# Split heads of a decay attention: two TensorE passes for the products with v in place of three, row sums on VectorE, squares on ScalarE

## Chip, core and metric

The kernel runs on one core of a Trainium2 chip. A core has a matrix engine (TensorE, PE in the profile, with its weight loads as PEld), a vector engine (VectorE, DVE), an engine for pointwise functions (ScalarE, ACT), a general one (GpSimd, POOL) and one that issues transfers (SyncE, SP). Each works through its own queue in order; semaphores tie the queues together. Data lies in SBUF (128 partitions) or in PSUM, where TensorE writes its sums, eight banks of 128 x 512 fp32. The metric is the time of one execution in microseconds.

## Reference

Eight batches of eight heads, 576 positions of 64 values. Each head is causal attention whose scores get a decay: the difference of cumulated logarithms of f. The 4608 rows of 512 that come out go through a two-layer MLP with a squared relu.

```python
scores = scale * np.matmul(q, k.transpose(0, 1, 3, 2))
cum = np.cumsum(np.log(np.clip(f, 0.0001, 1.0)), axis=-1)
scores = np.where(causal, -1e9, scores + cum[:, :, :, None] - cum[:, :, None, :])
scores = scores - np.max(scores, axis=-1, keepdims=True)
attn = np.exp(scores)
attn = attn / (np.sum(attn, axis=-1, keepdims=True) + 1e-09)
x = np.matmul(attn, v)                 # heads side by side: 4608 x 512
h = np.maximum(x @ w_in, 0.0)          # 512 -> 2048
out = h * h @ w_out                    # 2048 -> 512
```

## The kernel before

**Precision.** Most products run in a faster fp32 format of TensorE (F32R) that rounds its operands. To keep the digits, an operand is split into a rounded upper part and a lower part, the rest: ph and pl for the exponentials p, vh and vl for v, xh and xl, gh and gl in the MLP. A product of two split operands takes three passes: upper by upper, upper by lower, lower by upper.

**Heads.** The first 14 heads (`NWHOLE`) multiply unsplit fp32; in that time the weights of the MLP are loaded and split. The other 50 are **split heads**. A head has six units (`UNITS`): blocks of 128 keys (64 for the last) against the queries that see them, with 320, 320, 192, 64, 448 and 256 queries. The loop at the end of the kernel goes through slots, one unit of one head each. In a slot stand, in this order, the score of the unit, the products with v of the unit two slots earlier (`LAG`), and whatever is due there: parts of the next head's preparation (`prep`, `split_v`), its row maxima (`max_units`), and halves of MLP steps, dealt out by `fill`. A half is `mlp1` (12 matmuls of 256 columns into bank 4) or `mlp2` (6 matmuls of 512). Most batches' heads get 64 halves for the 48 slots of eight heads, one batch's 96: four or six steps to a head.

**A unit's way.** `score` multiplies on TensorE and takes the exponential on ScalarE (p); GpSimd masks the block on the diagonal (L384; units 1 to 5 have one); `split_p` rounds p to ph on ScalarE (L397) and subtracts on VectorE to get pl (L398); `av_split` multiplies with v. The 576 queries are summed in two parts, upper (320 columns, units 0 to 4) and lower (256 columns, units 5 and 4), each in the same PSUM bank 0, one after the other. A part's last matmul is followed on ScalarE by a copy of x (L444) and one of the row sum den (L446), which comes from a column of ones in vh. When both have read the bank, the next sum may start there.

**Division.** `finish` spreads the row sums of two heads over the partitions by way of DRAM, inverts them on VectorE (L462, L463) and has GpSimd multiply x (L471).

**MLP step.** ScalarE takes the relu r (L509), VectorE squares it to g (L510), ScalarE squares it to gh, rounded (L511), VectorE subtracts to get gl (L512); `mlp2` uses them a step later. r and g have one buffer each.

**Order.** `in_order` ties every engine's instructions to the order in which the program writes them, SP's DMAs from the first slot on. So what an instruction waits for also holds up all that stands behind it on its engine.

## Time and profile before

| what | us |
|---|---|
| median of 3 runs | 1231.75 (1227.86 to 1232.46) |
| the profiled execution's own time | 1235.45 |
| its span, first to last instruction | 1233.7 |
| first score of a split head | 214.2 |
| stretch with MLP steps alone | from 1081.8 on |
| TensorE, VectorE, ScalarE, GpSimd busy in the span | 1185.7, 772.9, 701.1, 410.9 |

How to read the rows in what follows. A row of a timeline has start and duration in us, engine, line of the kernel, operation, tiles (written <- read), shapes, and in brackets how long the engine sat idle before it and what ended the wait. A row of groups has busy time and mean duration in ns, then the idle time before and its releasers. The row of a window has, for each engine, the busy time within it and the number of instructions, then TensorE's granted clock, the DMA share and GB/s. Matmuls overlap, so a matmul's cost is the distance from its start to the next one's, not its duration; an engine's other instructions overlap a little too.

### The profile page before, as it was taken

How to read it: one execution, taken by the hardware profiler on the slowest of the kernel's cores; microseconds unless marked ns; L12 is line 12 of the kernel's file. 1: busy time of each engine (PE TensorE's matmuls, PEld its weight loads, DVE VectorE, ACT ScalarE, POOL GpSimd, SP SyncE). 2: the span in 40 equal slices, each digit the busy share in tenths (PEclk: the TensorE clock that was granted, in tenths of full speed). 3: DMA queues.
4: the chain of work that ended last, by engine and by line, in shares of the span. 5: the costliest groups of instructions: out<-in, count | busy, mean ns of one | idle time of the engine just before them, and what ended most of it. 6: DMA issues, size and time to landing. Idle time of an engine off the chain costs nothing.

```text
span 1233.7 us, 23332 instructions
## 1 busy us (share of the span) xinstructions
PE 1185.7 (96%) x7652; PEld 1050.8 (85%) x7652; DVE 772.9 (63%) x2044; ACT 701.1 (57%) x1720; POOL 410.9 (33%) x670
## 2 busy tenths in 40 slices
PE   5876998999999999999999999999999999999998
PEld 3554887988999899999899989998999899999997
DVE  7666874667676767666655676667666667533332
ACT  3553664666666666665655666666666666633332
POOL 4554544433333333332222233334333434200000
PEclk9897998999999999999999999999999999999999
DMA  7776531112121212121102121211121212000000
GB/s 202 180 158 159 165 103 43 36 40 50 42 58 41 57 33 53 32 58 36 49 16 58 27 58 42 57 34 48 36 58 42 58 41 58 12 27 1 18 18 18
DMA packets 114977, 71.62 MB, mean 58 GB/s; under 512 B 96908, under 2 KB 96908, under 8 KB 114856
## 3 DMA queue, kind: packets, MB, share of 16 engines
q1 hardware_dynamic: 113736, 66.00, 21.7%
q0 software_dynamic: 1120, 4.13, 1.6%
q8 instruction: 61, 1.00, 0.4%
q14 instruction: 60, 0.49, 0.1%
HBM read 59.90 MB, written 9.87 MB: 57 GB/s over the span
## 4 chain that ended last, share of the span: by engine, by line
PE 64%; ACT 2%; issue 1%; POOL 1%; DVE 0%; DMA 0%; SPq 0%; POOLq 0%; DVEq 0%
PE bank L501 25%; PE bank L524 24%; PE bank L407 3%; PE bank L372 2%; PE bank L409 2%; PE bank L324 2%; PE bank L408 2%; PE bank L369 2%; ACT den L446 0%; ACT r L509 0%; ACT p L382 0%; DMA den<-rdr 0%; ACT ph L397 0%; POOL v L310 0%; ACT gh L511 0%
## 5 line engine op out<-in xcount | busy, mean ns | idle before, releaser
L524 PE MATMUL bank<-w,gh 128*128 128x512 f32 x1152 | 414.7, 401 | 0.0
L501 PE MATMUL bank<-xh,w 128*128 128x256 f32 x2304 | 331.8, 287 | 2.8 <-DVE tcol L330 2.2
L501 PEld LDWEIGHTS bank<-xh,w 128*128 128x128 f32 x2304 | 302.9, 190 | 11.3 <-DVE tcol L330 2.4
L398 DVE TENSOR_TENSOR pl<-p,ph 128x320 fp32r<-128x320 f32 (+4 forms) x300 | 182.2, 607 | 201.7 <-ACT ph L397 192.9
L524 PEld LDWEIGHTS bank<-w,gh 128*128 128x128 f32 x1152 | 217.7, 189 | 38.5
L524 PE MATMUL bank<-w,gl 128*128 128x512 f32 x576 | 227.1, 394 | 0.1
L509 ACT ACTIVATE r<-bank 128x256 f32<-128x256 f32 x288 | 110.5, 384 | 198.7 <-PE bank L501 185.7
L510 DVE TENSOR_TENSOR g<-r 128x256 f32<-128x256 f32 x288 | 129.1, 448 | 145.1 <-ACT r L509 144.4
L384 POOL TENSOR_SCALAR_AFFINE_SELECT p<-p 128x128 f32<-128x128 f32 (+1 forms) x250 | 81.3, 325 | 413.8 <-ACT p L382 273.4
L397 ACT CAST ph<-p 128x320 fp32r<-128x320 f32 (+4 forms) x300 | 124.5, 415 | 151.6 <-POOL p L384 149.8
L501 PE MATMUL bank<-xl,w 128*128 128x256 f32 x1152 | 185.1, 283 | 0.0
L501 PEld LDWEIGHTS bank<-xl,w 128*128 128x128 f32 x1152 | 159.0, 191 | 0.0
L330 DVE CUSTOM_DVE_ANT_0 bank<-bank,mz 128x256 f32<-128x256 f32 (+4 forms) x320 | 133.1, 433 | 35.3 <-PE bank L324 29.4
L382 ACT ACTIVATE p<-bank 128x320 f32<-128x320 f32 (+4 forms) x300 | 116.1, 387 | 63.1 <-PE bank L372 51.3
L512 DVE TENSOR_TENSOR gl<-g,gh 128x256 fp32r<-128x256 f32 x288 | 126.0, 438 | 35.1 <-PE bank L524 0.5
L324 PE MATMUL bank<-rk 66*128 66x320 f32 (+9 forms) x384 | 111.8, 322 | 22.9 <-DMA rk<-qkraw 9.9
L511 ACT ACTIVATE gh<-r 128x256 fp32r<-128x256 f32 x288 | 120.6, 419 | 9.1
L524 PEld LDWEIGHTS bank<-w,gl 128*128 128x128 f32 x576 | 109.3, 190 | 14.2 <-DVE gl L512 0.9
L210 POOL TENSOR_TENSOR w<-osb,w 128x128 fp32r<-128x128 f32 x128 | 72.7, 596 | 79.4 <-ACT w L206 42.3
L407 PE MATMUL bank<-pl,vh 128*65 128x320 f32 (+4 forms) x350 | 96.8, 277 | 2.4 <-ACT den L446 2.4
L324 PEld LDWEIGHTS bank<-rk 66*128 66x128 f32 (+3 forms) x384 | 69.8, 189 | 33.4 <-issue 13.1
L408 PE MATMUL bank<-ph,v 128*64 128x320 f32 (+4 forms) x350 | 94.7, 270 | 0.0
(82 smaller groups left out, 1560.9 us busy)
## 6 DMA issues: line engine op xcount, KB each, us to landing
qkraw<-in_qk SPq DMA_DIRECT2D x50, 288.0 KB
v<-in_v SPq DMA_DIRECT2D x62, 160.0 KB
out<-osb SPq DMA_DIRECT2D x36, 256.0 KB
den<-rdr SPq DMA_DIRECT2D x62, 144.0 KB
w<-in_w_in SPq DMA_DIRECT2D x16, 512.0 KB
w<-in_w_out SPq DMA_DIRECT2D x16, 512.0 KB
rk<-in_qk POOLq DMA_DIRECT2D x14, 288.0 KB, 5.0
rl<-in_qk SPq DMA_DIRECT2D x14, 288.0 KB
```

The source lines that it names most:

```text
L324: nc.tensor.matmul(ps[:m, :n], st["r2"][:rows, q0:q0 + m], st["kl0"][:rows, k0:k0 + n], start=True, stop=True,)
L330: nc.vector.tensor_tensor_reduce(out=ps[:m, :n], in0=ps[:m, :n], in1=mz[:m, mo:mo + n], op0=ALU.add, op1=ALU.min, scale=-1.0, scalar=init, ...
L382: nc.scalar.activation(out=p[:kn, :n], in_=ps[:kn, :n], func=AF.Exp, scale=SCALE)
L397: nc.scalar.copy(out=ph[:, :n], in_=p[:, :n])
L398: nc.vector.tensor_tensor(out=pl[:, :n], in0=p[:, :n], in1=ph[:, :n].bitcast(F32), op=ALU.subtract,)
L407: nc.tensor.matmul(acc[:D + 1, o], vh, pl[:, i], start=first, stop=False)
L408: nc.tensor.matmul(acc[:D, o], vl, ph[:, i], start=False, stop=False)
L501: nc.tensor.matmul(ph[:, :T], w[:, s, cc], x[:, cc, :], start=(cc == 0 and k == 0), stop=(cc == NCC - 1 and k == 2),)
L510: nc.vector.tensor_tensor(out=g, in0=r, in1=r, op=ALU.mult)
L511: nc.scalar.activation(out=gh, in_=r, func=AF.Square)
L512: nc.vector.tensor_tensor(out=gl, in0=g, in1=gh.bitcast(F32), op=ALU.subtract)
L524: nc.tensor.matmul(po, g[:, ts], w[:, s], start=(fc == 0 and k == 0), stop=(fc == NF - 1 and k == 2),)
```

## The change

In split heads the split v lies side by side in one tile of 128 columns, `vhl`: columns 0 to 63 the upper part, 64 to 127 the lower. One matmul of these 128 columns with ph gives upper by upper in partitions 0 to 63 of the bank and lower by upper in 64 to 127; a second one, of the upper 64 columns with pl, adds to the first 64. At the end ScalarE copies partitions 64 to 127 to x, and VectorE adds partitions 0 to 63 to it.

The column of ones has no room any more, so the row sums are taken on VectorE: `sum_p` adds each unit's p into one tile (wmag), and after the last unit a transposing reduce adds it up over groups of 32 partitions. `store_sums` and `finish` bring the four groups together by way of DRAM. In every MLP step g is squared on ScalarE. Tiles move for the space: v has two buffers in place of three, den one, and the whole heads' row sums go to a free row of qkraw.

```diff
@@ split_v @@
-            vh = st["vh"] = vhs[h % 2]
-            st["vl"] = wk.tile([P, NJ, D], F32R, name="v", bufs=3)
-            nc.vector.tensor_copy(out=vh[:, :, :D], in_=vr)
+            v = st["vhl"] = vhls[h % 2]
+            nc.vector.tensor_copy(out=v[:, :, :D], in_=vr)
             nc.gpsimd.tensor_tensor(
-                out=st["vl"], in0=vr, in1=vh[:, :, :D].bitcast(F32), op=ALU.subtract,
+                out=v[:, :, D:], in0=vr, in1=v[:, :, :D].bitcast(F32), op=ALU.subtract,
             )
@@ split_p @@
         st["p"][u] = ph, pl
+        sum_p(h, u, p)
+
+    def sum_p(h, u, p):
+        st = state[h]
+        _, q0, q1 = UNITS[u]
+        if u == 0:
+            st["sum"] = wk.tile([P, S], F32, name="wmag", bufs=1), q1
+        total, known = st["sum"]
+        if known < q1:
+            o = slice(max(q0, known), q1)
+            nc.vector.tensor_tensor(
+                out=total[:, o], in0=total[:, o], in1=p[:, o.start - q0:q1 - q0], op=ALU.add,
+            )
+        if q0 < known:
+            nc.vector.tensor_copy(out=total[:, q0:min(known, q1)], in_=p[:, :min(known, q1) - q0])
+        st["sum"] = total, min(known, q0)
+        if u == NU - 1:
+            st["sums"] = wk.tile([P, NC], F32, name="sums")
+            nc.vector.tensor_reduce(
+                out=st["sums"], in_=total.rearrange("p (i c) -> p c i", c=NC),
+                axis=mybir.AxisListType.X, op=ALU.add, apply_transpose=True,
+            )
+
+    def store_sums(h):
+        st, i = state[h], h % 2
+        st["sdr"] = state[h - 1]["sdr"] if i else dr.tile([4, D, NC], F32, name="sdr")
+        nc.sync.dma_start(out=st["sdr"][:, i * 32:(i + 1) * 32], in_=st["sums"])
@@ av_split @@
-        nc.tensor.matmul(acc[:D + 1, o], vh, pl[:, i], start=first, stop=False)
-        nc.tensor.matmul(acc[:D, o], vl, ph[:, i], start=False, stop=False)
-        nc.tensor.matmul(acc[:D + 1, o], vh, ph[:, i], start=False, stop=last)
+        vhl = st["vhl"][:, j]
+        high = acc[:, o], vhl, ph[:, i]
+        low = acc[:D, o], vhl[:, :D], pl[:, i]
+        for k, args in enumerate((high, low) if first else (low, high)):
+            nc.tensor.matmul(*args, start=first and k == 0, stop=last and k == 1)
@@ av_part @@
+            if h >= NWHOLE:
+                nc.scalar.copy(out=x, in_=acc[D:, :n])
+                nc.vector.tensor_tensor(out=x, in0=x, in1=acc[:D, :n], op=ALU.add)
+                return
             nc.scalar.copy(out=x, in_=acc[:D, :n])
@@ finish @@
+            if h >= NWHOLE:
+                nc.sync.dma_start(
+                    out=st["cmp"].rearrange("p (g c) -> p g c", g=4),
+                    in_=st["sdr"].rearrange("g p c -> p g c"),
+                )
@@ mlp1 @@
         nc.scalar.activation(out=r, in_=ph[:, :T], func=AF.Relu)
-        nc.vector.tensor_tensor(out=g, in0=r, in1=r, op=ALU.mult)
+        nc.scalar.activation(out=g, in_=r, func=AF.Square)
         nc.scalar.activation(out=gh, in_=r, func=AF.Square)
@@ slots @@
+            at((h + 1) * NU, 1, store_sums, h)
```

Names keep their meaning; line numbers grow, so that L309 (cast of v) becomes L312, L310 (its lower part) L313, L398 (pl) L401, L444 (copy of x) L481, L512 (gl) L570. L416 and L420 are the adds and copies of `sum_p`, L425 its reduce, L482 the add from PSUM.

VectorE around the end of a split head, before: from pl of unit 4 to pl of the next head's unit 0.

```order
L398 TENSOR_TENSOR pl<-p,ph 128x448
L309 CAST vh_73<-v 128x5x64
L398 TENSOR_TENSOR pl<-p,ph 128x256
L510 TENSOR_TENSOR g<-r 128x256
L512 TENSOR_TENSOR gl<-g,gh 128x256
L290 CAST rk_68<-qkraw 64x576
L291 CAST rk_68<-qkraw 64x576
L398 TENSOR_TENSOR pl<-p,ph 128x320
```

The same place in VectorE's queue with the change:

```order
L401 TENSOR_TENSOR pl<-p,ph 128x448
L416 TENSOR_TENSOR wmag<-wmag,p 128x320
L420 COPY wmag<-p 128x128
L312 CAST vhl_73<-v 128x5x64
L401 TENSOR_TENSOR pl<-p,ph 128x256
L416 TENSOR_TENSOR wmag<-wmag,p 128x128
L420 COPY wmag<-p 128x128
L425 TENSOR_REDUCE sums<-wmag 128x18
L570 TENSOR_TENSOR gl<-g,gh 128x256
L482 TENSOR_TENSOR xt_9325<-xt_9325,bank_10166 64x320
```

The cast of v now stands behind an add and a copy, and the first add from PSUM behind a copy, an add and the reduce of unit 5. GpSimd's queue is as it was: the lower part of v, then the mask of unit 5.

ScalarE from the rounding of a head's unit 5 to the copy that reads the bank of the lower part, before:

```order
L397 CAST ph<-p 128x256
L509 ACTIVATE r<-bank_10187 128x256
L511 ACTIVATE gh<-r 128x256
L382 ACTIVATE p<-bank_10214 128x320
L444 COPY xt_9222<-bank_10051 64x320
L446 COPY den<-bank_10051 1x320
L292 CAST rl<-qkraw 64x576
L397 CAST ph<-p 128x320
L509 ACTIVATE r<-bank_10235 128x256
L511 ACTIVATE gh<-r 128x256
L382 ACTIVATE p<-bank_10256 128x320
L444 COPY xt_9222<-bank_10262 64x256
```

ScalarE's queue there with the change, from the first relu on:

```order
L567 ACTIVATE r<-bank_10307 128x256
L568 ACTIVATE g<-r 128x256
L569 ACTIVATE gh<-r 128x256
L385 ACTIVATE p<-bank_10334 128x320
L481 COPY xt_9325<-bank_10166 64x320
L296 CAST rl<-qkraw 64x576
L400 CAST ph<-p 128x320
L567 ACTIVATE r<-bank_10357 128x256
L568 ACTIVATE g<-r 128x256
L569 ACTIVATE gh<-r 128x256
L385 ACTIVATE p<-bank_10378 128x320
L481 COPY xt_9325<-bank_10384 64x256
```

Two squares (L568) have come into this stretch and one den copy (L446) has left it; a second den copy has left from behind the last row, and in its stead VectorE's L482 is the last to read the bank.

More of the change, by code (lines that the diff above doesn't have):

```diff
@@ L112, in decay_attention_relu2_kernel @@
     whole = [wk.tile([P, 2, S], F32, name="rl") for _ in range(2)]
-    vhs = [cpool.tile([P, NJ, D + 2], F32R, name=f"vh_{i}") for i in range(2)]
+    vhls = [cpool.tile([P, NJ, P], F32R, name=f"vhl_{i}") for i in range(2)]
+    qkraw = cpool.tile([P, 2, S], F32, name="qkraw")
+    NC = S // 32
     def f32(x):
@@ L237, in load @@
     def load(h):
-        raw = wk.tile([P, 2, S], F32, name="qkraw", bufs=1)[:D]
+        raw = qkraw[:D]
         nc.sync.dma_start(out=raw, in_=qk[h])
@@ L470, in finish @@
             x = xts[h // H][:, (h % H) // 2, :]
-            nc.gpsimd.tensor_tensor(out=x, in0=x, in1=den, op=ALU.mult)
+            nc.gpsimd.tensor_tensor(out=x, in0=x, in1=st["den"], op=ALU.mult)
             del state[h], state[h - 1]
@@ L678, in decay_attention_relu2_kernel @@
     store_cum()
-    for x in vhs:
-        nc.gpsimd.memset(x[:, :, D:D + 2].bitcast(F32), 1.0)
     at(-3, 1, load_whole, 1)
```

45 lines of the change are left out of this document (28 added, 17 removed).

## The prediction

> **What bounds the kernel now.** I read the page's busy line first, then the table of windows, then the timelines of a few heads, engine by engine.
>
> ```profile
> PE 1185.7 (96%) x7652; PEld 1050.8 (85%) x7652; DVE 772.9 (63%) x2044; ACT 701.1 (57%) x1720; POOL 410.9 (33%) x670
> 740.00:864.00 124.00, 123.51 (x842) 112.24 (x841) 84.61 (x238) 80.19 (x201) 47.11 (x73) 1.00 0.20 46
> ```
>
> TensorE is busy all through the mixed phase, VectorE for about two thirds of it: by the averages TensorE is the bound, and the change takes work from TensorE. But the averages hide how tight the hand-offs are. The 50 split heads start here (first score matmul of a head):
>
> ```profile
> 547.54 0.31 PE L369 MATMUL bank<-rk 67*128 67x320 f32 x1
> 718.86 0.31 PE L369 MATMUL bank<-rk 67*128 67x320 f32 x1
> 735.80 0.31 PE L369 MATMUL bank<-rk 67*128 67x320 f32 x1
> 735.96 0.31 PE L372 MATMUL bank<-rl 128*128 128x320 f32 x1
> 752.06 0.31 PE L369 MATMUL bank<-rk 67*128 67x320 f32 x1
> ```
>
> Eight heads lie between the first two rows of L369, 21.4 us each: **long heads**, with six MLP steps to a head. The head from 735.80 took 16.26 us, a **short head** with four steps; 42 of the 50 are of that kind. The head from 718.86 is a short one too, and took 16.94. Why it lost 0.68 us is the key to this change. In it TensorE waited for a PSUM bank:
>
> ```profile
> 724.42 0.36 PE L407 MATMUL bank<-pl,vh 128*65 128x320 f32 x1 [0.39 <-ACT den L446]
> 740.66 0.36 PE L407 MATMUL bank<-pl,vh 128*65 128x320 f32 x1
> ```
>
> Products with v accumulate in one bank, and a new sum can start only when the old one is read out. In the normal short head the next sum began 4.86 us after the head's first score (740.66 - 735.80), in the other 5.56 us (724.42 - 718.86). What made it late stands on ScalarE and GpSimd:
>
> ```profile
> 717.85 0.89 POOL L310 TENSOR_TENSOR v<-v,vh 128x320 fp32r<-128x320 f32 x1 [1.88 <-PE bank L501]
> 719.33 0.38 ACT L509 ACTIVATE r<-bank 128x256 f32<-128x256 f32 x1
> 719.74 0.42 ACT L511 ACTIVATE gh<-r 128x256 fp32r<-128x256 f32 x1
> 720.06 0.42 ACT L382 ACTIVATE p<-bank 128x320 f32<-128x320 f32 x1
> 720.51 0.42 ACT L444 COPY xt<-bank 64x320 f32<-64x320 f32 x1
> 720.94 0.42 ACT L446 COPY den<-bank 1x320 f32<-1x320 f32 x1
> 721.26 0.67 ACT L292 CAST rl<-qkraw 64x576 fp32r<-64x576 f32 x1
> ...
> 723.63 0.36 ACT L444 COPY xt<-bank 64x256 f32<-64x256 f32 x1
> 724.00 0.36 ACT L446 COPY den<-bank 1x256 f32<-1x256 f32 x1
> 750.17 0.88 POOL L310 TENSOR_TENSOR v<-v,vh 128x320 fp32r<-128x320 f32 x1 [1.67 <-PE bank L407]
> 751.64 0.38 ACT L509 ACTIVATE r<-bank 128x256 f32<-128x256 f32 x1
> ```
>
> From the relu at 719.33 ScalarE works without a gap to the copy at 724.00, which frees the bank: 5.09 us from that relu to TensorE's start at 724.42. In the normal head from 752.06 the same relu starts at 751.64, 0.42 us ahead of the head; in the late one 0.47 us after it. The relu is late because GpSimd's split of v was: 1.01 us before the head (717.85) in place of 1.89 (750.17). The mask of the last unit is queued behind that split, the rounding to ph behind the mask, the relu behind the rounding. So 0.88 us at the split of v became 0.89 us at the relu and 0.68 us of the head. That is a price list for delays at this place.
>
> **The change, part by part.** *TensorE.* One of three matmuls goes in each of seven parts of a head. Its price is the distance to the next start, not its duration:
>
> ```profile
> 736.25 0.31 PE L408 MATMUL bank<-ph,v 128*64 128x320 f32 x1
> 736.40 0.31 PE L409 MATMUL bank<-ph,vh 128*65 128x320 f32 x1
> 747.07 0.25 PE L408 MATMUL bank<-ph,v 128*64 128x192 f32 x1
> 747.16 0.25 PE L409 MATMUL bank<-ph,vh 128*65 128x192 f32 x1
> ```
>
> 0.15 us for 320 columns and 0.09 for 192 are 0.47 ns a column; a head's parts have 3x320 + 256 + 192 + 128 + 64 = 1600 columns, so 0.75 us a head and **37.5 us** over 50 heads. Weights of 128 columns in place of 65 I cost at nothing: L369, which has them, stands 0.16 us ahead of L372 (735.80, 735.96), at the same 320 columns. This is what the change can win.
>
> *ScalarE.* The square g comes to it (one more instruction in each MLP step), two den copies a head go. From row to row of the chain above, a square takes 0.32 us (719.74 to 720.06), a den copy 0.32 (720.94 to 721.26) or 0.36.
>
> *VectorE.* The squares leave it; a head gets five adds, three copies and one transposing reduce for the row sums, and two adds that finish x from PSUM. Nearest rows:
>
> ```profile
> L510 DVE TENSOR_TENSOR g<-r 128x256 f32<-128x256 f32 x288 | 129.1, 448 | 145.1 <-ACT r L509 144.4
> 738.83 0.49 DVE L398 TENSOR_TENSOR pl<-p,ph 128x320 fp32r<-128x320 f32 x1
> 749.13 0.62 DVE L398 TENSOR_TENSOR pl<-p,ph 128x448 fp32r<-128x448 f32 x1 [0.75 <-ACT ph L397]
> 749.68 0.35 DVE L309 CAST vh<-v 128x320 fp32r<-128x320 f32 x1
> L489 DVE TENSOR_TENSOR xl<-xt,xh 128x512 fp32r<-128x512 f32 x4 | 2.8, 693 | 0.1
> L290 DVE CAST rk<-qkraw 64x576 fp32r<-64x576 f32 x50 | 27.7, 555 | 0.0
> L454 DVE RECIPROCAL den<-den 128x576 f32<-128x576 f32 x1 | 3.8, 3753 | 0.0
> L330 DVE CUSTOM_DVE_ANT_0 bank<-bank,mz 128x256 f32<-128x256 f32 x64 | 27.1, 423 | 22.3 <-PE bank L324 17.6 <-DMA rl<-in_qk 4.5 <-issue 0.2
> ```
>
> An add of 320 columns takes 0.49 us, shorter ones in proportion: some 1.8 us a head, the copies 0.7 (a cast of 320 takes 0.35), the adds from PSUM 0.9 (0.42 for 256 columns). No row has a transposing reduce; it reads 576 columns, so it lies between the cast (0.56) and the reciprocal (3.75). I take 0.78, the subtraction's rate at 512 columns (0.693 us), since it too reads one element after another. [...] VectorE's new work is then 4.2 us a head against 1.8 us of squares (4 x 0.448) taken away: 2.4 us more, in a short head that has 5.2 us of idle VectorE (39.4 of 124 us in the window above). VectorE does not become the bound by its sum; what matters is where in its queue the work stands.
>
> *That place.* The head's last units put an add and a copy between pl of unit 4 and the cast of v (749.13, 749.68), and the cast releases GpSimd's split of v. That is just the place priced above. The step's relu is followed by one more square, too, ahead of unit 4's exp: 0.32 us. Sum up to the relu: -0.42 us now; TensorE reaches the head 0.12 us earlier (parts of 192 and 64 columns, 256 at 0.47 ns), so -0.30; the square +0.32; the add +0.45; the copy of 128 columns +0.15. The relu starts 0.62 us after the head begins, a little later than in the head of 718.86.
>
> *The chain from there* was 5.09 us. Two squares more are +0.64, the first den copy less -0.36. At its end the second den copy and its hand-off (0.79 us from 723.63 to 724.42, less the copy's 0.37) give way to VectorE's add from PSUM: 0.42 and two hand-offs of 0.05, so +0.1. That makes 5.47. The bank is free 6.09 us after the head begins; now the next sum starts at 4.86. From there to the next head TensorE needs 16.26 - 4.86 = 11.40 us, less 0.42 for the four removed matmuls there (896 columns): 10.98. The new short head is **17.07 us**, 0.8 longer than now, though TensorE has 0.75 us less to do. VectorE must also have done the first add from PSUM by the time the head's second unit is to be accumulated; by the rows it is late there by about 0.3 us, which is inside the wait counted above and adds nothing.
>
> *Long heads* keep the saving, since the bank has over two us to spare:
>
> ```profile
> 704.94 0.37 ACT L446 COPY den<-bank 1x256 f32<-1x256 f32 x1
> 707.55 0.31 PE L407 MATMUL bank<-pl,vh 128*65 128x320 f32 x1
> ```
>
> The den copy ended at 705.31, the next sum began at 707.55; 1.3 us of delay fits.
>
> *At no cost:* the last stretch, MLP steps alone, where ScalarE has 0.32 us more in a step and half its time free; the row sums' way through DRAM (75 small DMAs in place of 50 on SP's queue, with two slots between the read and its use; behind them stand the columns of maxima, and each us by which those came late would be one of TensorE before a head's first score); v in two buffers (its load waits for the head before last, a whole head before it is needed; behind it in SP's queue are weights, staged four ahead; between nothing and one slot, 2.7 us, in all).
>
> **Sum.** 42 x 0.8 = +34 us, less 8 x 0.75 = 6: +28 us. Since some short heads already lose 0.3 to 0.7 us at this same bank, I take a little less, +26. The profiled execution took 1235.45 us (its span 1233.7), so 1261; the runs' median is 1231.75, 3.7 lower, so **1257 us**.
>
> **Rivals.** (1) *TensorE remains the bound.* For it: the busy 96%, and idle VectorE ahead of the very place, 0.75 us in the row of 749.13. The lateness at the bank would have to vanish: ScalarE would have to start the relu before the rounding of unit 5, which its order forbids. It decides where the bank is free 4.53 us after the head's start (4.86 less 704 removed columns). Then all 37.5 us are won: 1194. Chance 0.17. (2) *Half the lateness:* if the add and copy ahead of the cast fit in VectorE's idle time, the relu starts at 0.02 and the head lasts 16.47: +0.2 x 42 - 6 = +3, with a span from 1215 to 1240. Chance 0.23. (3) *VectorE is held up more.* [...]
>
> ```profile
> 745.21 1.42 POOL L301 TENSOR_TENSOR rl<-qkraw,rl 64x576 fp32r<-64x576 f32 x1
> 745.95 0.75 DVE L398 TENSOR_TENSOR pl<-p,ph 128x64 fp32r<-128x64 f32 x1
> ```
>
> A 64-column subtraction takes 0.75 us here and ends just behind GpSimd's. The new adds can be caught by the multiply with 1/den (1.4 us, every second head), or the reduce may be nearer to the reciprocal. With 0.7 us more in a short head: +29, 1286, and beyond. Chance 0.12. [...] (4) *The third pass isn't saved:* weights of 128 columns slow the matmuls that remain, and the loss stands without the gain, 1290. Chance 0.03. The forecast, 1240 to 1280, has 0.45.
>
> **How the numbers follow.** A measurement of this kernel tells about 0.5% from no change: 1226 to 1238. Faster: rival 1 and 0.07 of rival 2, 0.24. Same: 0.13 of rival 2. Slower: the rest, 0.63. The range of 8 in 10 runs from 1198 to 1285: it leaves out half of rival 1 and most of 3 and 4. The likeliest case alone has 1240 to 1280.
>
> **What would show it.** In the new profile: short heads near 17 us, long ones near 20.7; the low part's copy and VectorE's add ending about 6 us after a head's first score; TensorE's longest waits in the mixed phase before matmuls with v, released by VectorE; the relu of the step before starting after the head has begun; two matmuls a part, 0.15 us apart. The reduce near 0.78 us. It is wrong if short heads last 15.5 us, if the split of v starts as early as now, or if TensorE waits at the score (columns of maxima late) rather than at the bank.

## The result, and the profile after

The changed kernel takes 1314.18 us (median of 4 runs, 1312.03 to 1318.16) beside 1230.84 for the one before in the same job: a ratio of 1.0681, 95% interval 1.0657 to 1.0705. The forecast was 1257, with a range to 1285. The sign is right, the size is not: 83 us are lost where 25 were expected.

The profiled execution took 1315.49 us (span 1313.8). Its busy line, and two windows of the mixed phase (the columns are those of the window shown above):

```profile
PE 1196.1 (91%) x7302; PEld 1041.4 (79%) x7302; DVE 891.0 (68%) x2331; ACT 747.0 (57%) x1908; POOL 411.0 (31%) x668
740.00:864.00 124.00, 113.45 (x720) 100.11 (x719) 98.04 (x261) 75.75 (x199) 42.11 (x64) 0.99 0.19 44
864.00:987.00 123.00, 110.27 (x674) 97.25 (x674) 95.22 (x252) 70.58 (x185) 42.13 (x62) 0.94 0.18 41
```

TensorE now has gaps of 10.5 us in the first window, where it had 0.5, and VectorE is still no more than 79% busy. No engine is full: something waits. The timeline of TensorE shows in which heads. First score matmuls of heads 45 to 49:

```profile
801.66 0.31 PE L372 MATMUL bank<-rk 67*128 67x320 f32 x1
820.43 0.31 PE L372 MATMUL bank<-rk 67*128 67x320 f32 x1
837.42 0.31 PE L372 MATMUL bank<-rk 67*128 67x320 f32 x1
858.10 0.31 PE L372 MATMUL bank<-rk 67*128 67x320 f32 x1
875.06 0.31 PE L372 MATMUL bank<-rk 67*128 67x320 f32 x1
```

The even heads (46, 48) last 16.99 and 16.96 us, as forecast (17.07). The odd ones (45, 47) last 18.77 and 20.68. The distances between the first scores of all split heads, sorted into four kinds, account for the loss ("behind a batch" are heads 17, 25, 33, 41, 49 and 57, in which the finished batch's x is split for the MLP):

| kind (number) | before, us in all | after | difference | forecast |
|---|---|---|---|---|
| even short heads (21) | 345.4 | 360.1 | +14.7 | +17 |
| odd short heads (15) | 244.9 | 292.9 | +48.0 | +12 |
| behind a batch (6) | 105.8 | 131.0 | +25.2 | +5 |
| long heads (7) | 152.4 | 148.9 | -3.5 | -5 |

With the opening (the first split score at 208.9 in place of 214.2) and the stretch from the last head on (171.9 for 171.0) this is the whole 80 us between the spans. The forecast was near the number in the first and the last row (28 of 49 distances) and missed the two middle ones by 56 us.

Three of TensorE's waits, summed by what ended them (us, number, longest):

```profile
PE bank L444 <- DVE xt L482: 52.4, 56, 2.1
PE bank L559 <- ACT r L567: 10.5, 39, 0.8
PE bank L327 <- DVE rk L295: 3.9, 5, 1.2
```

L482 is VectorE's add from PSUM, the last to read the bank. How long does it take itself? Two lines over the whole execution (ns: shortest, median, longest):

```profile
L482 DVE TENSOR_TENSOR xt<-xt,bank x100: 402/444/483, 227.5 to 1161.5; 64x320 f32<-64x320 f32 x50, 64x256 f32<-64x256 f32 x50
L570 DVE TENSOR_TENSOR gl<-g,gh x288: 379/425/1639, 116.7 to 1308.3; 128x256 fp32r<-128x256 f32 x144
```

The add never takes over 0.48 us; gl, which stands right ahead of it in VectorE's queue, takes up to 1.64. The timeline of odd head 47 (from 837.42), VectorE, GpSimd and TensorE:

```profile
840.31 0.47 DVE L482 TENSOR_TENSOR xt<-xt,bank 64x320 f32<-64x320 f32 x1
840.71 0.44 DVE L294 CAST rk<-qkraw 64x576 fp32r<-64x576 f32 x1
841.08 1.68 DVE L295 CAST rk<-qkraw 64x576 fp32r<-64x576 f32 x1
842.68 0.60 DVE L401 TENSOR_TENSOR pl<-p,ph 128x320 fp32r<-128x320 f32 x1
843.21 0.31 DVE L420 COPY wmag<-p 128x320 f32<-128x320 f32 x1
843.45 1.61 DVE L570 TENSOR_TENSOR gl<-g,gh 128x256 fp32r<-128x256 f32 x1
844.99 0.40 DVE L482 TENSOR_TENSOR xt<-xt,bank 64x256 f32<-64x256 f32 x1
...
840.96 1.48 POOL L529 TENSOR_TENSOR xt<-xt,den 128x576 f32<-128x576 f32 x1 [3.41 <-DMA den<-rdr]
842.92 1.86 POOL L302 TENSOR_TENSOR rl<-qkraw,rk 64x576 fp32r<-64x576 f32 x1
...
845.54 0.39 PE L444 MATMUL bank<-ph,vhl 128*128 128x320 f32 x1 [2.13 <-DVE xt L482]
```

And the same place in even head 48 (from 858.10):

```profile
858.57 0.38 ACT L567 ACTIVATE r<-bank 128x256 f32<-128x256 f32 x1
...
861.63 0.38 PE L444 MATMUL bank<-ph,vhl 128*128 128x256 f32 x1 [0.64 <-DVE xt L482]
...
862.98 0.41 DVE L570 TENSOR_TENSOR gl<-g,gh 128x256 fp32r<-128x256 f32 x1
863.45 0.42 DVE L482 TENSOR_TENSOR xt<-xt,bank 64x256 f32<-64x256 f32 x1
...
863.52 1.43 POOL L302 TENSOR_TENSOR rl<-qkraw,rk 64x576 fp32r<-64x576 f32 x1
...
864.01 0.39 PE L444 MATMUL bank<-ph,vhl 128*128 128x320 f32 x1
```

The cast L295 and the subtraction L570, both from SBUF to SBUF, began while a GpSimd operation ran and ended 0.3 us behind it (842.76 behind 842.44, 845.06 behind 844.78): they were **locked out** by it. From 214 us on, 14 gl of this trace began while L302 ran and took 1.61 to 1.64 us, the 198 that met no GpSimd operation 0.38 to 0.43. In the odd head a lock stands twice ahead of the low part's add: the multiply with 1/den (L529, once for two heads, so in odd heads alone) catches a cast of k, 1.68 us in place of 0.44; the queue is then so late that the lower part of k on GpSimd (L302) catches gl too, 1.61 in place of 0.41. Together 2.4 us. In the even head L302 begins at 863.52, when gl is done. The next sum started 8.12 us after the head in the one (forecast 6.09), 5.91 in the other.

Two things in this are easily missed. The first lock is older than the change: in the kernel before, too, the multiply caught a cast of k in 11 heads, all odd, and it cost nothing. This is head 47 of the kernel before, which lasted 16.27 us:

```profile
802.09 1.69 DVE L291 CAST rk<-qkraw 64x576 fp32r<-64x576 f32 x1
```

New is the second lock: gl ahead of the low part's add took over 1.6 us in 13 of the 15 odd short heads, in none before; the other two lasted 17.5 us. And in even head 48 TensorE does not wait at the next sum at all. Its wait is the 0.64 us at 861.63, where the sum of the low part starts behind the upper part's add. In 20 of the 21 even heads it stands there (12.9 us in all), and 7.2 us are waits for the relu.

After the long waits of odd heads comes a second loss. Head 45's wait, and windows of heads 47 and 45 (the granted clock is the third number from the end):

```profile
809.44 0.38 PE L444 MATMUL bank<-ph,vhl 128*128 128x320 f32 x1 [1.95 <-DVE xt L482]
```

```profile
842.76:846.17 3.41, 1.28 (x8) 1.07 (x8) 3.41 (x7) 1.83 (x5) 2.52 (x3) 1.00 0.00 0
846.17:849.59 3.42, 3.42 (x16) 3.28 (x15) 1.52 (x7) 0.81 (x3) 0.15 (x1) 0.50 0.02 0
849.59:853.00 3.41, 3.41 (x25) 3.12 (x25) 2.66 (x9) 0.81 (x4) 1.66 (x2) 1.00 0.02 0
...
805.21:808.62 3.41, 2.28 (x13) 1.86 (x13) 3.41 (x5) 3.13 (x9) 2.59 (x3) 1.00 0.03 3
808.62:812.04 3.42, 2.60 (x18) 2.53 (x19) 2.98 (x10) 0.84 (x4) 0.66 (x3) 1.00 0.00 0
```

In this trace and in that of the kernel before the granted clock changes only at steps of 3.413 us, on a grid that lies elsewhere in each. Head 47's wait of 2.13 us lies whole within one interval of that grid; TensorE was busy for 1.28 us of that interval, and the next one ran at one half, with 16 matmuls in place of the 25 of the one behind it. At that clock it costs 3.41 x 0.5 = 1.7 us, an estimate from the window. Head 45 had waited 1.95 us at the same matmul, but the step at 808.62 cuts its wait in two, and the clock stayed at 1.00. These 1.7 us are most of the difference between the two heads (20.68 and 18.77). The length of the wait alone does not decide: heads 51, 55 and 61 waited 1.84 to 1.85 us and have an interval at half clock as well. In this trace, from 205 us on, each of the 13 full-clock intervals with TensorE busy for 0.59 to 1.78 us was followed by one at half clock, none of the 293 with 1.85 us or more; in the kernel before, none of 299, the least busy with 2.02 us (ends of matmuls are modelled, so these times are rough). Why the clock falls there is not shown.

The stretch of the split heads as a whole, after and before:

```profile
208.89:1141.88 932.99, 858.41 (x5392) 763.26 (x5391) 716.26 (x1884) 560.09 (x1447) 306.16 (x465) 0.97 0.18 42
214.16:1062.70 848.54, 843.72 (x5733) 768.60 (x5732) 568.44 (x1539) 536.90 (x1334) 303.14 (x466) 1.00 0.19 45
```

The changed kernel has 16 intervals at half clock there, the one before has none. That is up to 27.3 us, a third of the 83: 15.4 in odd short heads, 11.9 in those behind a batch. Of the 13 odd heads with gl caught, the five that kept the clock lasted 18.7 to 19.0 us, the other eight 20.2 to 21.2.

### The profile page after: what moved, and what is told of

Same layout as the page of the kernel before. It is cut to its first block, busy times and chain, and to the rows that moved or that the text cites. A ratio compares the mean times of both kernels' runs of the same rounds, so it can differ in the third digit from the quotient of the medians.

```text
span 1313.8 us, 22758 instructions
## 1 busy us (share of the span) xinstructions
PE 1196.1 (91%) x7302; PEld 1041.4 (79%) x7302; DVE 891.0 (68%) x2331; ACT 747.0 (57%) x1908; POOL 411.0 (31%) x668
## 4 chain that ended last, share of the span: by engine, by line
PE 61%; DVE 13%; issue 9%; ACT 5%; POOL 5%; DMA 0%; DVEq 0%; POOLq 0%; SPq 0%; ACTq 0%
PE bank L559 25%; PE bank L582 22%; PE bank L444 5%; PE bank L327 3%; DVE gl L570 3%; POOL vhl L313 2%; DVE xt L482 2%; PE bank L375 2%; PE bank L372 2%; ACT ph L400 2%; DVE pl L401 1%; DVE wmag L420 1%; DVE rk L294 1%; DVE bank L333 1%; POOL rl L305 1%
## 5 line engine op out<-in xcount | busy, mean ns | idle before, releaser
L582 PE MATMUL bank<-w,gh 128*128 128x512 f32 x1152 | 420.0, 405 | 0.0
L559 PE MATMUL bank<-xh,w 128*128 128x256 f32 x2304 | 341.8, 292 | 14.0 <-ACT r L567 10.5
L559 PEld LDWEIGHTS bank<-xh,w 128*128 128x128 f32 x2304 | 307.7, 195 | 31.2 <-ACT r L567 20.9
L570 DVE TENSOR_TENSOR gl<-g,gh 128x256 fp32r<-128x256 f32 x288 | 146.7, 509 | 219.5 <-ACT gh L569 218.6
L401 DVE TENSOR_TENSOR pl<-p,ph 128x320 fp32r<-128x320 f32 (+4 forms) x300 | 174.8, 583 | 129.1 <-ACT ph L400 128.0
L387 POOL TENSOR_SCALAR_AFFINE_SELECT p<-p 128x128 f32<-128x128 f32 (+1 forms) x250 | 86.1, 345 | 427.3 <-ACT p L385 187.9
L444 PE MATMUL bank<-ph,vhl 128*128 128x320 f32 (+4 forms) x350 | 110.0, 314 | 59.3 <-DVE xt L482 52.4
L444 PEld LDWEIGHTS bank<-ph,vhl 128*128 128x128 f32 x350 | 66.3, 189 | 78.6 <-DVE xt L482 38.4
L568 ACT ACTIVATE g<-r 128x256 f32<-128x256 f32 x288 | 120.3, 418 | 10.6 <-DVE gl L570 1.5
L569 ACT ACTIVATE gh<-r 128x256 fp32r<-128x256 f32 x288 | 115.7, 402 | 0.0
```

The source lines that it names most:

```text
L401: nc.vector.tensor_tensor(out=pl[:, :n], in0=p[:, :n], in1=ph[:, :n].bitcast(F32), op=ALU.subtract,)
L444: nc.tensor.matmul(*args, start=first and k == 0, stop=last and k == 1)
L559: nc.tensor.matmul(ph[:, :T], w[:, s, cc], x[:, cc, :], start=(cc == 0 and k == 0), stop=(cc == NCC - 1 and k == 2),)
L568: nc.scalar.activation(out=g, in_=r, func=AF.Square)
L569: nc.scalar.activation(out=gh, in_=r, func=AF.Square)
L570: nc.vector.tensor_tensor(out=gl, in0=g, in1=gh.bitcast(F32), op=ALU.subtract)
```

## The experiments

Three theories. **Queue theory:** what counts is when VectorE, in its order, reaches the add from PSUM, and which GpSimd operations lock it out on the way. **Load theory:** VectorE has too much work in a head, wherever it stands. **Clock theory:** TensorE's lower clock is the cause, not a consequence. All results in one table; each job had its own runs of the kernel before (1229.5 to 1230.4). The last columns are median lengths of a head in us, by kind.

| run | edit | us | ratio to before (95%) | even | odd | behind a batch | long |
|---|---|---|---|---|---|---|---|
| before | | 1230.8 | | 16.26 | 16.25 | 17.52 | 21.72 |
| after | the change | 1314.2 | 1.0681 (1.0657-1.0705) | 16.99 | 20.18 | 21.67 | 21.11 |
| e1 | two banks for the sums | 1294.7 | 1.0534 (1.0460-1.0607) | 17.38 | 18.05 | 19.85 | 21.09 |
| e2 | multiply and steps 2 slots later | 1269.4 | 1.0328 (1.0260-1.0396) | 16.99 | 16.86 | 17.92 | 21.11 |
| e3 | before + squares on ScalarE | 1258.2 | 1.0237 (1.0167-1.0307) | 17.00 | 16.87 | 17.00 | 21.72 |
| e4 | after, squares on VectorE | 1380.4 | 1.1231 (1.1157-1.1305) | 20.38 | 18.98 | 21.97 | 22.08 |
| e5 | v split 1 slot earlier | 1250.7 | 1.0168 (1.0144-1.0192) | 15.98 | 16.56 | 22.29 | 21.11 |
| e6 | L302 1 slot later | 1277.2 | 1.0379 (1.0349-1.0408) | 16.96 | 17.73 | 19.16 | 21.10 |
| e7 | no row sums | 1258.2 | 1.0226 (1.0201-1.0252) | 16.45 | 16.63 | 21.39 | 21.13 |
| e8 | reduce behind the add | 1304.2 | 1.0601 (1.0577-1.0625) | 16.95 | 17.65 | 24.03 | 21.11 |
| e9 | e5, x split 1 slot later | 1231.7 | 1.0014 (0.9996-1.0031) | 15.97 | 16.55 | 18.19 | 21.11 |
| e10 | e9 + edit of e2 | 1298.9 | 1.0569 (1.0537-1.0600) | 17.48 | 16.63 | 17.76 | 21.11 |
| e11 | e10, L296 later | 1299.2 | 1.0568 (1.0538-1.0597) | 17.49 | 16.54 | 18.07 | 21.11 |
| e12 | e11, L302 later | 1321.3 | 1.0737 (1.0707-1.0768) | 17.45 | 17.76 | 20.14 | 21.11 |
| e13 | multiply alone later | 1279.7 | 1.0404 (1.0369-1.0439) | 16.97 | 17.08 | 22.18 | 21.11 |
| e14 | steps alone later | 1300.4 | 1.0567 (1.0539-1.0596) | 17.10 | 17.58 | 19.74 | 21.11 |
| e15 | e5 + edits of e13 | 1240.1 | 1.0079 (1.0053-1.0105) | 15.97 | 16.09 | 21.39 | 21.11 |
| e16 | e9, L296 later | 1244.9 | 1.0129 (1.0084-1.0174) | 15.80 | 16.57 | 18.87 | 21.11 |
| e17 | e9, multiply later within a batch | 1224.7 | 0.9951 (0.9933-0.9968) | 15.98 | 16.09 | 18.01 | 21.11 |
| e18 | e17, L296 later | 1224.5 | 0.9951 (0.9937-0.9965) | 15.72 | 15.71 | 18.29 | 21.10 |

### What kind of bound: e1, e3, e4

e1 gives the sums of products with v a second bank, taken from the scores and maxima:

```diff
-banks.update(s=[1, 2, 3, 5], m=[], av=[0])
+banks.update(s=[1, 2, 3], m=[], av=[0, 5])
```

> The changed kernel with two PSUM banks for the products with v (0 and 5 in turn) and three in place of four for the scores. Queue theory: TensorE waits because the one bank is read out late, VectorE's add from PSUM standing behind casts and gl that GpSimd's multiply holds up. With a second bank that wait goes: even heads 16.95 us to about 15.9 (the wait for the relu stays), odd heads 18.7 to 21.4 us to about 17; whole kernel 1225 to 1260, with whatever three score banks cost in it. Load theory (VectorE simply has too much work, 96 of 123 us busy in the mixed phase): its work is the same, the heads stay long, over 1295. Clock theory (wider matmuls lower TensorE's granted clock): the clock row stays at 0.94 to 0.96 and the time over 1295.

1294.66: missed by the queue theory's number. Odd heads got 2.1 us shorter, but the wait took another place. TensorE's longest entry in e1 is for the banks of the maxima:

```profile
PE bank L327 <- DVE tcol L333: 60.8, 48, 5.0
```

VectorE still reads its other inputs late, and with one bank less for them TensorE waits there. So a second bank taken from elsewhere is no cure; what a spare one would do is not shown.

e3 and e4 move the square g; e3 makes this edit on the kernel before, e4 its reverse on the changed one:

```diff
-nc.vector.tensor_tensor(out=g, in0=r, in1=r, op=ALU.mult)
+nc.scalar.activation(out=g, in_=r, func=AF.Square)
```

> The kernel before with one part of the change alone: g squared on ScalarE. Queue theory: one square more ahead of unit 5's relu and two in the chain to the bank, so the bank comes free about 0.8 us later in each short head: 16.25 to 17.0 us, long heads as before, whole kernel 1255 to 1268. Rival, that ScalarE at 57% busy hides them: 1228 to 1238.

> The changed kernel with g squared on VectorE again. Queue theory: ScalarE's chain to the bank gets 0.64 us shorter and the relu 0.3 us earlier, but VectorE has two squares more ahead of its adds from PSUM, 0.35 us each, and is then the last: even heads 16.7 to 17.2 us, odd ones as they are; 1295 to 1325. Load theory: 129 us more on the engine that bounds, of which some 100 in split heads, so 1350 to 1400.

e3, 1258.21: as expected. The squares alone make a short head 0.6 to 0.7 us longer, and long heads not at all; TensorE's wait in them (0.67 us in head 48) is for the second den copy, at the end of ScalarE's chain. e4, 1380.4, missed by a good 55 us, and it hit the load theory's number. Its trace shows the lock of head 47 in even heads too: with one more instruction in VectorE's queue, L302 (at 832.60, 1.48 us) catches the square there, 1.63 us. So more work does cost more here, by way of a lock; the load theory needed runs that leave the amount as it is.

### What makes odd heads long: e2, e6, e13, e14

e2 has the first of these edits, e6 the second. e13 has the first and the third, which keeps the MLP steps at their slots (the split of x, which needs the product, goes two slots later with the multiply):

```diff
-DIVIDE = (2, 6, 9, 13), (2, 4, 6, 7)
+DIVIDE = (2, 6, 9, 13), (2, 4, 6, 9)
...
-SPLIT = 0, 1, 1, 3
+SPLIT = 0, 1, 2, 3
...
-ready = [fin(b * H + H - 1, 3) + 2 for b in range(B)]
+ready = [fin(b * H + H - 1, 3) + (2 if b == 0 else 0) for b in range(B)]
-at(ready[b] - 1 - (b > 0), 0, split_x, ...)
+at(ready[b] - (b == 0), 0, split_x, ...)
```

e14 leaves DIVIDE and the split of x where they were and puts the steps two slots later:

```diff
-ready = [fin(b * H + H - 1, 3) + 2 for b in range(B)]
+ready = [fin(b * H + H - 1, 3) + (2 if b == 0 else 4) for b in range(B)]
-at(ready[b] - 1 - (b > 0), 0, split_x, ...)
+at(ready[b] - 1 - 3 * (b > 0), 0, split_x, ...)
```

> The changed kernel with GpSimd's multiply by 1/den two slots later (part 3 of the division at 9 in place of 7), away from the casts and from gl. Queue theory: odd heads lose what sets them apart from even ones and come to 17 to 17.5 us; 21 x 3 us, so 1245 to 1270, and the granted clock returns to 1.00 as the waits of two us go. Load theory: no engine has less work, so no change, 1300 or more. Clock theory: no change.

> The changed kernel with one GpSimd operation, the lower part of k (L302, 1.4 to 1.9 us), one slot later, behind the mask of unit 2. Queue theory: in odd short heads gl (L570, 1.61 us in head 47 in place of 0.41) is no longer caught ahead of the low part's add from PSUM, so they lose some 1.2 us; the lock falls on later instructions that TensorE needs less; even heads as before; total 1275 to 1300. If the multiply with 1/den alone makes odd heads long: no change, 1305 to 1320. If the lock only moves to pl of the next units, and TensorE waits there: 1300 to 1330.

> The changed kernel with the multiply with 1/den two slots later, and the MLP steps kept at the slots that they had (in e2 they moved with it). If the multiply's lock on VectorE makes odd heads long: odd heads 16.8 to 17.5 as in e2, total 1255 to 1280. If e2 won by the steps' new place against the heads: odd heads stay at 18.7 to 21, total 1300 to 1325.

> The changed kernel with each batch's MLP steps beginning two slots later, the multiply where it was: the other half of e2. If the multiply makes odd heads long: 1300 to 1330, no better than the changed kernel. If the steps' place does: 1255 to 1285.

The totals of e2 and e6 came out as the queue theory has them; e6's odd heads got 2.5 us shorter where 1.2 were expected, since their half-clock intervals went as well. But e2's later multiply also moved the start of each batch's MLP steps. e13 and e14 part the two. With the multiply alone later odd heads fall from 20.18 to 17.08, 36.6 us in all (292.9 to 256.3), just what the forecast missed there. The timeline of e13's odd head 47 (from 817.90), VectorE and GpSimd:

```profile
821.55 0.45 DVE L295 CAST rk<-qkraw 64x576 fp32r<-64x576 f32 x1
822.67 0.42 DVE L570 TENSOR_TENSOR gl<-g,gh 128x256 fp32r<-128x256 f32 x1
823.39 0.41 DVE L482 TENSOR_TENSOR xt<-xt,bank 64x256 f32<-64x256 f32 x1 [0.29 <-ACT xt L481]
...
823.34 1.42 POOL L302 TENSOR_TENSOR rl<-qkraw,rk 64x576 fp32r<-64x576 f32 x1
```

Neither the cast nor gl is locked out: without the first lock L302 comes too late to make the second. In e6 the first lock remains and gl is free (0.41 us at 828.01), in e8 the casts are free and the multiply meets gl (1.47 us at 840.84); both have odd heads of some 17.7. Two locks, one, none: 20.2 (18.8 where the clock held), 17.7, 17.1. The load theory falls with this, since no work is taken away. So does the clock theory as a first cause: e6 lost 3.4 us to the clock in its split heads, in place of 27.3 (granted clock of the whole run 0.988, of the changed kernel's 0.970), and is still 47 us slower than the kernel before. As a consequence of the waits the clock counts: of the 36.6 us that e13 won in odd heads, 15.4 are intervals at half clock that no longer occur.

e14, 1300.35, lies near the edge of what the multiply theory gave it and shows that the steps' place matters too (14 us less than the changed kernel, the intervals apart): odd heads get better, some even ones worse, up to 21.75. Which instruction meets which there stays open.

### What makes the queue late: e5, e7, e8

e5 has the first of these edits, e7 the second (`ones` is a constant), e8 the third (`reduce_p` is the reduce of `sum_p`, `sum_first` its call for unit 0):

```diff
-VLOAD, VSPLIT = 2, 4
+VLOAD, VSPLIT = 1, 3
...
-sum_p(h, u, p)
-nc.sync.dma_start(out=st["sdr"][:, i * 32:(i + 1) * 32], in_=st["sums"])
+nc.sync.dma_start(out=st["sdr"][:, i * 32:(i + 1) * 32], in_=ones[:, :NC])
...
+at(h * NU + 1, 0, sum_first, h)
+at((h + 1) * NU + 1, 0, reduce_p, h)
-at((h + 1) * NU, 1, store_sums, h)
+at((h + 1) * NU + 1, 1, store_sums, h)
-DIVIDE = (2, 6, 9, 13), (2, 4, 6, 7)
+DIVIDE = (2, 6, 9, 13), (3, 5, 6, 7)
```

> The changed kernel with v loaded and split one slot earlier, so that the cast of v (L312) and GpSimd's lower part of v no longer stand behind the add and copy of unit 4, nor the mask of unit 5 behind them. In head 48 of the changed kernel p of unit 5 was there at 855.83 and masked only at 857.92, so the relu (858.57) and all behind it on ScalarE and VectorE can start 1 to 2 us earlier. Queue theory (what counts is when VectorE reaches its add from PSUM, and which GpSimd operations lock it out on the way): short heads of both parities get shorter, even ones 15.6 to 16.5, odd ones 16 to 18.5, total 1235 to 1280. Load theory (the amount of VectorE's work sets the head, wherever it stands): over 1300, since nothing is taken away.

> The changed kernel without the row sums on VectorE (left out: the adds and copies of sum_p and the transposing reduce; a constant goes to DRAM in their place, the transfers stay). Queue theory: the relu is no longer late by the add and copy ahead of the cast of v (0.6 us), and the reduce (1.26), add and copy no longer stand ahead of the add from PSUM; even short heads 16.2 to 16.6 (ScalarE's two squares remain), odd ones 16.5 to 17.5; total 1225 to 1260, still no better than the kernel before. Load theory: 3.8 us of VectorE's work a head less, and all of it is won in short heads: 1160 to 1200.

> The changed kernel with the same instructions, the transposing reduce and the first copy of a head's row sums moved behind the low part's add from PSUM (reading and inverting the sums one slot later, the multiply where it was). Queue theory: the upper and the low add come 1.2 us earlier in VectorE's queue, and the casts of k are done before the multiply with 1/den begins, so that one lock is missed in odd heads: odd short heads 16.8 to 18, even ones 16.6 to 17.1 (ScalarE's chain stays), total 1240 to 1280. Load theory: the same work, over 1300.

e5, 1250.71, takes 63 us off by moving one cast and one subtraction of v, with the amount of work unchanged: the mask of unit 5 no longer stands behind GpSimd's split of v, so relu, squares and VectorE's queue come earlier; the casts of k are through when the multiply starts (780.68 and 780.78 in head 45), so that one lock of two is left. Even heads fall below those of the kernel before, odd ones to 0.3 us above. e7, 1258.15, within the queue theory's range: even without any row sum on VectorE this kernel is slower than the one before. Its even heads, 16.45, are 0.54 us shorter; the forecast had 0.60 for the add and the copy ahead of the cast, but since the reduce goes too, e7 tests no single term. e8, 1304.20, a miss: odd heads fell as expected, but heads behind a batch grew to 24.03 and took the gain back. Its even heads stayed at 16.95. With the reduce out of the way TensorE no longer waits for the upper part's add, but for the low part's (10.6 us in 20 even heads): the two paths are equally long there, and taking one away leaves the other.

### Behind a batch's end: e5 again, and e9

In e5 these heads are the only ones that are still much longer than before. Its head 49 began at 842.87 and lasted 22.7 us. VectorE and TensorE there, and two windows:

```profile
847.01 0.56 DVE L546 CAST xh<-xt 128x768 fp32r<-128x768 f32 x1 [2.04 <-POOL xt L529]
848.84 0.45 DVE L295 CAST rk<-qkraw 64x576 fp32r<-64x576 f32 x1
849.34 0.39 PE L327 MATMUL bank<-rk 66*128 66x256 f32 x1 [2.16 <-DVE rk L295]
851.94 0.60 PE L444 MATMUL bank<-ph,vhl 128*128 128x320 f32 x1 [2.01 <-POOL p L387]
```

```profile
849.00:853.00 4.00, 1.65 (x7) 1.47 (x8) 4.00 (x9) 0.68 (x2) 1.96 (x3) 0.76 0.00 0
853.00:866.00 13.00, 13.00 (x74) 11.73 (x73) 9.18 (x27) 6.54 (x17) 3.27 (x5) 0.81 0.22 65
```

The split of x (L546) waits 2.04 us for the multiply, the casts of the next head's k stand behind it, and TensorE's maxima wait for these; a second wait follows, and the clock is at one half from 851.11 to 857.94 (the windows' 0.76 and 0.81 are means). e9 writes the split of x one slot later:

```diff
-at(ready[b] - 1 - (b > 0), 0, split_x, b * S // T, b + 1)
+at(ready[b] - 1, 0, split_x, b * S // T, b + 1)
```

> The split of v one slot earlier as in e5, and the split of a finished batch's x for the MLP (L546, L547) one slot later, so that it no longer waits on VectorE for GpSimd's multiply with 1/den while the casts of the next head's k stand behind it. In e5 (1250.71) five heads after a batch's end lasted 4.9 to 6.3 us longer than in the kernel before, with two waits of 2 us and a granted clock of 0.76 to 0.81 behind them. Queue theory: those heads fall to 16.5 to 19, 27 us in all; the other heads stay at 15.97 and 16.55; total 1218 to 1235. If those heads are long for another reason (loads of v, a tight PSUM bank): 1245 to 1255.

1231.68, as expected: these six heads fell from 132.6 us to 110.6 in all; up to 15.4 of these 22 us are the nine half-clock intervals of e5, of which e9 has none (granted clock of the whole run 0.975 in e5, 0.986 in e9). With two slots changed the kernel is level with the one before (ratio 1.0014, 0.9996 to 1.0031).

### Putting it together: e10 to e12, e15 to e18

e10 is e9 with e2's edit of DIVIDE. e11 adds the first edit below, which moves ScalarE's copy of k (L296) from part 0 of `prep` to part 1, and e12 adds e6's SPLIT to that. e15 is e5 with e13's edits, e16 is e9 with the copy of k moved. e17 is e9 with the second edit, in `fin`: the multiply comes two slots later, but for each batch's last pair. e18 is e17 with the copy of k moved.

```diff
@@ prep @@
-            nc.scalar.copy(out=st["l2"][D:], in_=st["raw"][:, 1, :])
         st = state[h]
         if part == 1:
+            nc.scalar.copy(out=st["l2"][D:], in_=st["raw"][:, 1, :])
@@ fin @@
-        return (h + 1) * NU - 1 + (DIRECT if replicated(h) else DIVIDE[h >= H])[part]
+        return (h + 1) * NU - 1 + (DIRECT if replicated(h) else DIVIDE[h >= H])[part] + (
+            2 if part == 3 and h >= NWHOLE and h % H < H - 1 else 0
+        )
```

> e9 with the multiply with 1/den two slots later as in e2, where VectorE has maxima to take from PSUM. Queue theory: odd heads lose the lock of gl (L570, 1.29 us in e5's head 45 in place of 0.43) ahead of the low add and get as long as even ones, 16.0: 21 x 0.55, 11 us less than e9, 1205 to 1225. Load theory (odd heads longer because the multiply must be done at some time): as e9.

> e10 with ScalarE's copy of k (L296, 0.67 us) out of the chain between the two copies from PSUM, one slot later. In e5's even head 44 ScalarE ran without a gap from the exponential of unit 0 (762.38) to the low part's copy (ended 766.20), and TensorE waited 0.27 us for the add behind it. Queue theory: this wait goes, short heads 15.6 to 15.8, total 1195 to 1215. If TensorE itself is the bound by then at 15.97: as e10.

> e11 with the lower part of k (L302) one slot later as in e6. Queue theory: with the low add no longer late, L302 comes after it anyway (766.18 in e5's head 44, the add at 766.23), so this moves only the lock on pl of unit 1: within 6 us of e11. If L302's place still mattered as in the changed kernel, 20 us or more less than e11.

All three missed: e10 and e11 by over 70 us, and e12 came out 22 us above e11. Odd heads did fall in e10 and e11, but even ones rose to 17.5, every second of them to 20 and more, since e2's edit moves the steps. Even head 46 of e10 (from 804.78), rows of ScalarE, VectorE and TensorE:

```profile
803.84 1.05 ACT L588 COPY osb<-bank 128x512 f32<-128x512 f32 x2
804.78 0.40 ACT L385 ACTIVATE p<-bank 128x256 f32<-128x256 f32 x1
807.98 0.25 DVE L546 CAST xh<-xt 128x256 fp32r<-128x256 f32 x1
809.06 0.48 DVE L482 TENSOR_TENSOR xt<-xt,bank 64x320 f32<-64x320 f32 x1
809.60 0.39 PE L444 MATMUL bank<-ph,vhl 128*128 128x256 f32 x1 [2.32 <-DVE xt L482]
```

The copies of a finished chunk's output now stand ahead of unit 5's exponential, and the next chunk's split of x ahead of the add. That is the same place made late by other work.

> e9 (v split earlier) with the multiply two slots later and the steps where they were. Multiply theory: the odd heads' 16.55 falls to the even ones' 15.97, 21 x 0.55 = 11 us less than e9, 1215 to 1226. If the multiply does as much harm at its new place: 1228 to 1245. If e10's 1299 came from the multiply and not from the steps: over 1280.

> e9 with ScalarE's copy of k (L296, 0.67 us) one slot later, out of the chain to the low part's copy. If ScalarE's chain is what even heads wait for (0.27 us in head 44): even heads 15.6 to 15.75, odd ones unchanged (a lock of gl decides there), 5 to 8 us less than e9, 1222 to 1228. If TensorE or VectorE is the bound by then: within 2 us of e9, 1229 to 1234.

> e9 with the multiply with 1/den two slots later, but for the last pair of each batch, whose multiply and split of x stay as in e9. If the account is complete (what is left are locks and waits at single places, which add up): odd short heads 16.0 to 16.1 as in e15, heads behind a batch's end 17.5 to 18.6 as in e9, 16 heads x 0.5 = 8 us less than e9, 1220 to 1227, faster than the kernel before by some 0.6%. If the lateness moves on to another place: 1229 or more.

> e17 with ScalarE's copy of k one slot later as in e16. If only the multiply spoiled e16 (heads of 17.4 to 19.4 among those of 15.71): even heads 15.7, odd ones 15.7 to 16.1, 5 to 10 us less than e17, 1212 to 1222. If ScalarE's copy does harm at its new place by itself: 1225 to 1245.

e15 missed its total and hit its mechanism: odd heads 16.09, but those behind a batch 21.39, because the split of x waits for the later multiply again. e16 missed: half of its even heads reached 15.7, but four rose to 17.4 to 18. e17 takes the better half of each: odd heads 16.09, those behind a batch 18.01, 1224.7 us. Its window of 740 to 864:

```profile
740.00:864.00 124.00, 119.74 (x793) 108.77 (x793) 113.36 (x289) 85.40 (x219) 50.31 (x71) 1.00 0.21 48
```

In that window VectorE is busier than in the changed kernel (113.36 us for 98.04), and the heads are shorter: the load theory's last ground is gone. e17 is 0.5% faster than the kernel before, 0.9951 (0.9933 to 0.9968), which is small but clear of 1, and 89 us faster than the changed one, with every part of the change in it. e18 brings most short heads to 15.7, yet five of 17.5 appear, and its time is e17's (missed: 1212 to 1222 was expected). In all five L302 catches gl again; here in head 42 (from 706.18), GpSimd and VectorE:

```profile
710.26 1.49 POOL L302 TENSOR_TENSOR rl<-qkraw,rk 64x576 fp32r<-64x576 f32 x1
710.39 1.64 DVE L570 TENSOR_TENSOR gl<-g,gh 128x256 fp32r<-128x256 f32 x1
```

What makes VectorE's queue 0.8 us later in these five than in the heads of 15.7 stays open.

## Why the prediction was right in sign and wrong in size

**Right.** *TensorE's saving* is real: two matmuls a part, long heads 0.61 us shorter (0.75 forecast), and in e18 15.71 in a short head, 0.54 below the kernel before. Rival 1's 15.5 was never reached in full. *The bank as the place* of the longest waits, released by VectorE: 52.4 us of waits. *The length of even heads*, 17.07 forecast: 16.99; the relu 0.47 us after the head's start (0.62 forecast), the next sum at 5.91 (6.09). The place of the wait was another, though: not the next sum, at the end of ScalarE's chain, but the sum before it, behind the upper part's add, 0.64 us. The forecast had VectorE "late there by about 0.3 us", and the reduce came out 0.48 us longer than it reckoned. That this wait "adds nothing" held all the same: e8 moved the reduce away, the wait went to the low part, and the heads kept 16.95. e3 shows ScalarE's chain at work by itself: with the squares as the only change, TensorE's wait (0.67 us in head 48) stands at its end. So the sum followed one of two paths that happen to be equally long; that the reduce did not make the other one longer is luck.

**The step that failed** is "VectorE does not become the bound by its sum; what matters is where in its queue the work stands", carried out for one place in that queue only. The forecast followed VectorE up to the cast of v; the path to the add from PSUM it followed on ScalarE, with "0.42 and two hand-offs of 0.05" at its end, and put VectorE "late there by about 0.3 us". What stands ahead of the low part's add on VectorE (the reduce, two casts, a copy, gl) was priced as if never late and never locked out; in odd heads it was late by 2.4 us of locks in head 47. Then one price, 0.8 us, was put on all 42 short heads. And the granted clock stands in no term of the sum, which puts its loss at nothing; up to 27.3 us went there.

**The lock** was there as rival 3, with the right GpSimd operation (the multiply, every second head), a chance of 0.12 and 0.7 us a short head. It measured 36.6 us over 15 odd heads (e13), 2.4 a head, of which 1.0 is the clock's. Three things were not seen: that the multiply's lock was there before the change and harmless, so that what counts is a late queue behind it; that one lock makes the next (L302 catches gl only because the queue before it was late; e6, e8, e13); and that a wait of about 2 us that lay within one interval of the clock's grid (2.13 us in head 47) was followed by 3.4 us at half clock.

**Behind a batch** the forecast had nothing beyond the 0.8 us of every short head. e9's one slot took 22 us off e5 there, clock and all. That the multiply, the split of x and the casts of k form one chain there stood in the code, and it costs more when the chain starts later: these heads were 1.3 us longer than others before, 4.7 longer than even ones after.

**The reduce** took 1.26 us, not 0.78: 0.48 us a head too little, in the very queue that decides. 50 of them between 1254 and 1261 ns, 11 of which ran beside a multiply of GpSimd, for 0.01 to 1.26 us: none was lengthened. It took 2.18 ns a column (1.258 us for 576) where the subtraction whose rate the author took over had 1.35 (0.693 us for 512).

**The last stretch**, priced at nothing, took 0.9 us more.

## What to carry to other kernels

When work moves to an in-order engine with idle time, list what will stand ahead of each instruction that another engine waits for, and put beside it the other engine's operations that can lock it out; idle time in the sum says nothing about either. Locks can come in chains: here one delay of 1.24 us (1.68 for 0.44) moved the queue under the next GpSimd operation. A wait can be paid twice, once as itself and once in the clock: 2.13 us and an estimated 1.7 in head 47. The cure here was not less work, but moving three pieces of it (the splits of v and x, the multiply) by a slot or two, away from the place where the queue is tight.

## What was not expected of the hardware

A cast from SBUF to SBUF, with one input, was locked out by GpSimd like the subtraction with two: 1.68 us in place of 0.44; the row shown with rival 3 was a subtraction's, and the forecast had no such cast. The add with one input from PSUM never was: 402 to 483 ns over 100, 19 of which began while L302 or L529 ran and ended 0.87 us or more before it. The transposing reduce of 576 columns took 1.26 us; a subtraction of 512 took 0.69 before. And the clock: an interval of the 3.41 us grid with 1.28 us of work was followed by one at half clock, while a wait of 1.95 us that a step of the grid divides (2.28 and 2.60 us of work beside it) left it at 1.00.
